# Reordering the end of block 0 in a retention + feed-forward kernel: weight loads, held input loads, a state moved between engines, and one state earlier in block 2

## The chip, the core and the metric

The kernel runs on one core of one Trainium2 chip. The metric is the device time of one execution in microseconds. The core has TensorE (matmuls; PE in the profile, PEld for its weight loads), VectorE (DVE), ScalarE (ACT), GpSimd (POOL), and SyncE (SP), which here only issues transfers.

## What is computed

Eight batches of retention (attention with a decaying causal weight in place of a softmax), followed by a feed-forward layer with a "snake" activation over all 4608 tokens:

```python
scores = scale * np.matmul(q, k.transpose(0, 1, 3, 2))      # (8, 8, 576, 576), head size 64
Dmat = np.where(rel >= 0, gamma[:, None, None] ** rel[None, :, :], 0.0)
ret = scores * Dmat[None, :, :, :]
attn = np.matmul(ret, v)                                     # -> x: (4608, 512)
h = x @ w_in                                                 # 512 -> 2048
s = np.sin(alpha * h)
g = h + s * s / (alpha + 1e-09)
out = g @ w_out                                              # 2048 -> 512
```

Inputs and output are float32; the kernel computes its products in float16 and adds in float32.

## The kernel before, in words

**Attention of a batch `b` (class `Attention`).** The first 512 of a batch's 576 positions are taken in two parts p of 256 positions, each of two chunks of 128. For each part q, k and v are loaded (`load`, 512 KB each, issued by SyncE), scaled by the decay and cast to float16 (`cast`, L181 for q and k, L104 or L102 for v), and q and k are transposed, either by TensorE (`turn`, L215, into a PSUM bank) with a copy out of the bank (`take`, L102/L104), or by a transfer (`crossed`, L205, issued by SyncE). Inside a chunk the kernel forms decayed scores (`scores`, L363; `masked`, L375, on VectorE) and multiplies them by v (`values`, L406). Across chunks it carries a state: `outer` (L298) forms k-times-v sums in a bank, `evict`, `evict_bank` or `take_sum` (L102/L104) copies them to the float32 tile `kvs`, `more(c)` (L344, L345, two GpSimd instructions) adds the decayed sum before to the sum c, and `to_state(c)` (L332) makes the float16 state that `add_states` (L428) multiplies by q. `next_sum` (L327), four VectorE instructions that decay and add straight out of the bank, stands in the class and isn't used before the change. The tile `kvs` has a single buffer for all batches: batch 4's sums can't be copied in before batch 3's last state is read. `keep` (L102/L104) writes the result as x, transposed, to the tile `xT`.

**Feed-forward of a block n (512 tokens, mostly batch n).** `project(n, fc)` (L541) makes 128 of the 2048 hidden features in a PSUM bank, four matmuls of 512 columns, or eight of 256 when it is called for halves. `sine` (L549, ScalarE), `square` (L558 on ScalarE, L560 on the others) and `product` (L565, VectorE) turn it into the tile `gT`; `product` is the last reader of the bank. `gemm2(n, u)` (L587) makes a quarter `u % 4` of the second product for 128 tokens `u // 4`: four matmuls that need four features of `gT` and quarter `u % 4` of w_out. `finish` copies the result out (`osb`) and stores it. From block 2 on the second product is formed with seven products of halves instead of eight (class `Quarters`, L658), for which `weigh` (L608, GpSimd) adds and subtracts halves of w_out beforehand.

**What sets the order.** The program is written out by hand, and each engine runs its instructions in that order, waiting on semaphores for what they read and for buffers to come free. The order of blocks 0 to 2 is a list of calls (L747 to L1271); later blocks are a loop. PSUM has the banks `h0`, `h1`, `h2`, `op` (one bank each) and `m0`, `m1` (two each). A tag names the bank that a call takes, and the call waits until the last user has read it. `told(instruction, engine)` puts a no-operation into an engine's queue that waits for that instruction; all that is behind it on the engine waits too. `relay=A_` of `values` does the same on ScalarE between two groups of matmuls that write different rows of one bank.

w_in and w_out come by four transfers each, issued by GpSimd (`load_w_in`, `load_w_out`, L92 and L95), which also cast them to float16. The stretch around the change: block 0's features 0 to 15 are projected from 17.5 to 33.2 us, its second product stands between batch 1's attention from 33.2 to 51.9, and block 1's projections begin at 51.9 with the rest of block 0's second product and batch 2's attention in between. `raw` float32 tiles rotate through six buffers, so that a load of batch 2 also waits for the cast of the same place in batch 1.

Of the kernel before, what the change touches and what calls it, by code (L numbers as in the profile page):

```python
# [18 lines left out]
def kernel(  # L19
# [16 lines left out]
    nc = tc.nc  # L36
# [57 lines left out]
    def load_w_out(g):  # L94
        nc.gpsimd.dma_start(w_out16[:, 4 * g : 4 * g + 4, :], w_out_r[:, 4 * g : 4 * g + 4, :])  # L95
# [42 lines left out]
    def cast(b, nm, p, eng, ys=(0, 1)):  # L138
        t_ = raw[b, nm, p]
        if (b, nm, p) not in half:  # L140
            if p < 2:
                if nm == "k":
                    d_ = work.tile([P, 16 * D], F16, tag=f"k16{slot(b, p)}", bufs=1, name="k16")
                elif nm == "q":
                    n = order_of_q.index((b, p)) % 3 if b < 5 else 1 - p
                    d_ = work.tile([P, 16 * D], F16, tag=f"q16{n}", bufs=1, name="q16")
                else:
                    d_ = work.tile([P, 16 * D], F16, tag="v16", bufs=4, name="v16")
                d_ = (
                    d_.rearrange("p (h r d) -> p h r d", r=2, d=D)  # L150
                    if nm == "v"
                    else d_.rearrange("p (a r t d) -> p a r t d", a=4, r=2, t=2)
                )
            elif nm == "v":
                d_ = work.tile([P, H, D], F16, tag="vs16", bufs=B // 2, name="vs16")
            else:
                tag, n = ("qks16", 2) if b % 4 == 0 else (f"k16{int(nm == 'q')}", 1)
                d_ = work.tile([P, 4, 2, D], F16, tag=tag, bufs=n, name=nm + "s16")
            half[b, nm, p] = d_
        dst = half[b, nm, p]  # L160
        if p == 2:
            if nm == "v":
                copy(eng, dst.rearrange("p h d -> p (h d)"), t_.rearrange("p h d -> p (h d)"))
            else:
                eng.tensor_tensor(
                    dst.rearrange("p a t d -> p t a d"),
                    t_.rearrange("p (t a) d -> p t a d", t=2),
                    fac_s[nm].rearrange("p (t a) -> p t a", t=2).unsqueeze(3).to_broadcast([P, 2, 4, D]),
                    MULT,
                )  # L170
        elif nm == "v":
            h0, h1 = 4 * ys[0], 4 * ys[-1] + 4
            copy(
                eng,
                dst[:, h0:h1].rearrange("p h r d -> p (h r d)"),
                t_[:, h0:h1].rearrange("p h x -> p (h x)"),
            )
        else:
            a0, a1 = 2 * ys[0], 2 * ys[-1] + 2
            n = 2 * (a1 - a0)  # L180
            return eng.tensor_tensor(  # L181
                dst[:, a0:a1].rearrange("p a r t d -> p t (a r) d"),
                t_.rearrange("p (t a) x -> p t a x", t=2)[:, :, a0:a1].rearrange("p t a (r d) -> p t (a r) d", r=2),
                fac["halved k" if nm == "k" and b >= HALVED else nm]
                .rearrange("p (t x) -> p t x", t=2)[:, :, 2 * a0 : 2 * a1]
                .unsqueeze(3)
                .to_broadcast([P, 2, n, D]),
                MULT,
            )
# [19 lines left out]
    def turn(b, nm, p, tag, ys=(0, 1)):  # L209
        if (b, nm, p) not in trs:  # L210
            trs[b, nm, p] = psum.tile([P, 1024], F16, tag=tag, bufs=1, name="tr")
        tr, x = trs[b, nm, p], half[b, nm, p]
        for a in range(2 * ys[0], 2 * ys[-1] + 2):
            for r in range(2):
                matmul(  # L215
                    tr[:, 256 * a + 128 * r : 256 * a + 128 * r + 128],
                    x[:, a, r].rearrange("p t d -> p (t d)"),
                    ident,
                    start=(a == 0 and r == 0), stop=True, is_transpose=True, skip_group_check=True,
                )  # L220
# [312 lines left out]
    def project(n, fc, tag, part=None):  # L533

        if n not in gT:
            gT[n] = work.tile([P, 2, FC, 256], F16, tag="gT", bufs=2, name="gT")
        if (n, fc) not in hps_of:
            hps_of[n, fc] = [bank(tag), None]
        cols = PART[part]
        for a in range(KT):  # L540
            matmul(  # L541
                hps_of[n, fc][0][:, cols], w_in16[:, a, fc * P : (fc + 1) * P], xs[n][:, a, cols],
                start=(a == 0 and part != 1), stop=(a == KT - 1), skip_group_check=True,
            )

    def sine(n, fc):
        hps = hps_of[n, fc][0]
        s_t = work.tile([P, 512], F16, tag="s", bufs=4, name="s_t")
        nc.scalar.activation(  # L549
            s_t, hps, mybir.ActivationFunctionType.Sin, bias=0.0, scale=alpha_t[:, fc : fc + 1],  # L550
        )
        hps_of[n, fc][1] = s_t

    def square(n, fc, eng):
        s_t = hps_of[n, fc][1]
        ss_t = work.tile([P, 512], F16, tag="ss", bufs=4, name="ss_t")
        if eng is nc.scalar:
            nc.scalar.activation(ss_t, s_t, mybir.ActivationFunctionType.Square)  # L558
        else:
            eng.tensor_tensor(ss_t, s_t, s_t, MULT)  # L560
        hps_of[n, fc][1] = ss_t
# [184 lines left out]
    with tc.manual_schedule():  # L746
# [139 lines left out]
        project(0, 10, "m0")  # L886
        sine(0, 10)
        square(0, 10, G_)
        load_w_out(2)
        told(cast(1, "k", 0, V, (1,)), G_)  # L890
        project(0, 11, "op")
        sine(0, 11)
# [4 lines left out]
        sine(0, 12)  # L897
        square(0, 12, G_)
        project(0, 13, "h0")
        turn(1, "k", 0, "m1")  # L900
        take(1, "k", 0, V, (0,))
        take(1, "k", 0, V, (1,))
        sine(0, 13)
        square(0, 13, A_)
        cast(1, "q", 0, G_)
        product(0, 12)
        product(0, 13)
        project(0, 14, "h1")
        sine(0, 14)
        square(0, 14, A_)  # L910
        project(0, 15, "m0")
        sine(0, 15)
        product(0, 14)
        square(0, 15, A_)
        product(0, 15)
        gemm2(0, 4, "op")
        gemm2(0, 12, "h2")
        turn(1, "q", 0, "m1")
        take(1, "q", 0, A_, (0,))
        take(1, "q", 0, V, (1,))  # L920
        gemm2(0, 0, "h0")
        at[0].to_state(3, G_)
        at[1].scores(0, 0, "m0")
        at[1].scores(0, 1, "m1")
        at[1].masked(0, 0)
        at[1].masked(0, 1)
        gemm2(0, 5, "op")
        cast(1, "v", 0, G_, (0,))
        cast(1, "v", 0, A_, (1,))
        load_w_out(3)  # L930
        gemm2(0, 13, "h2")
        load(2, "k", 1)
        load(2, "k", 0)
        load(2, "q", 0)
        cast(1, "k", 1, G_)
        at[1].outer((0,), "m0")
        at[1].evict((0,), A_)
        at[1].values(0, False, "m1", relay=A_)
        at[1].to_state(0, G_)
        gemm2(0, 1, "h0")  # L940
        gemm2(0, 6, "op")
        turn(1, "k", 1, "h1")
        cast(1, "q", 1, V)
        take(1, "k", 1, V)
        at[1].values(0, True)
        at[1].add_states(0)
        at[1].keep(0, A_)
        load(2, "v", 0)
        load(2, "v", 1)
        load(2, "q", 1)  # L950
        turn(1, "q", 1, "m0")
        take(1, "q", 1, V)
        at[1].more(1)
        at[1].to_state(1, G_)
        weigh(1, 0, G_)
        cast(1, "v", 1, A_)
        gemm2(0, 8, "h1")
        at[1].scores(1, 1, "m0")
        at[1].scores(1, 0, "m1")
        at[1].masked(1, 1)  # L960
        at[1].masked(1, 0)
        cast(2, "k", 1, V)
        cast(2, "k", 0, V)
        crossed(2, 0, "k")
        gemm2(0, 9, "h1")
        gemm2(0, 14, "h2")
        gemm2(0, 2, "h0")
        at[1].outer((1,), "m0")
        at[1].evict((1,), A_)
        at[1].more(2)  # L970
        at[1].to_state(2, G_)
        at[1].values(1, False, "m1", relay=A_)
        gemm2(0, 10, "h1")
        gemm2(0, 15, "h2")
        finish(0, 3)
        gemm2(0, 7, "op")
        at[1].values(1, True)
        at[1].add_states(1)
        at[1].keep(1, A_)
        weigh(1, 1, G_)  # L980
        finish(0, 1)
# [531 lines left out]
```

## Time and profile before

| | |
|---|---|
| median of 3 runs | 296.5 us (296.3 to 296.61) |
| the profiled execution's own time | 296.5 us |
| its span (first to last instruction) | 294.8 us |
| granted TensorE clock | 0.997 |
| busy: TensorE, VectorE, ScalarE, GpSimd | 282.2, 218.1, 211.0, 208.9 us |
| HBM read and written | 36.74 MB, 9.44 MB |

Times in the text count from the start of the span. A row of the timeline has start, duration, engine, line, operation, output<-inputs, shape and count, and in brackets the idle time of the engine just before it and whose end ended that. Matmuls overlap, so that the next group can begin some 0.16 us before the end that a row shows. A row of the chain has start, duration and what was waited for.

### The profile page before, as it was taken

Reading aid. Unit: us, or ns where it says so; the run is one execution under the profiler, and the core shown is the slowest. Engines: PE = TensorE matmul, PEld = TensorE weight load, DVE = VectorE, ACT = ScalarE, POOL = GpSimd, SP = SyncE. Lnnn points to the kernel's source line nnn. Section 1 sums busy time; section 2 is a strip of 40 time slices with the busy share of each in tenths; the row PEclk is TensorE's granted clock in tenths of the full one; section 3 lists DMA queues with packets and bytes.
Section 4 is the critical chain, followed back from the end, with each engine's and each line's share of the span. In section 5 each row is a group of like instructions: output and inputs, shape, how many; then the busy total and the mean of one; then the engine's idle time right before and its main releaser. Section 6 shows DMA issues by size and latency. Waiting matters only on the chain.

```text
span 294.8 us, 8767 instructions
## 1 busy us (share of the span) xinstructions
PE 282.2 (96%) x3611; PEld 184.9 (63%) x3611; DVE 218.1 (74%) x294; ACT 211.0 (72%) x342; POOL 208.9 (71%) x201
## 2 busy tenths in 40 slices
PE   7699999999999899999999999999999999999993
PEld 5474454676644566676666666666666666665782
DVE  3759978599965799989686967686777495747861
ACT  2859823985959798787778778787868879887600
POOL 4888878999999989999997799679916800460000
PEclk9999999999999999999999999999999999999998
DMA  7999999999998787978799884778756101311225
GB/s 222 293 250 221 240 263 317 240 211 326 165 210 275 114 181 178 282 164 194 182 257 154 181 231 115 93 162 181 141 125 162 38 3 38 72 38 26 59 47 119
DMA packets 119159, 49.89 MB, mean 169 GB/s; under 512 B 69824, under 2 KB 118096, under 8 KB 119120
## 3 DMA queue, kind: packets, MB, share of 16 engines
q1 hardware_dynamic: 114528, 45.04, 65.9%
q0 software_dynamic: 4224, 4.19, 8.5%
q8 instruction: 28, 0.46, 0.7%
q10 hardware_dynamic: 368, 0.11, 0.2%
q14 instruction: 11, 0.09, 0.1%
HBM read 36.74 MB, written 9.44 MB: 157 GB/s over the span
## 4 chain that ended last, share of the span: by engine, by line
PE 65%; POOL 17%; DMA 6%; DVE 5%; issue 2%; ACT 2%; SPq 0%; POOLq 0%; DVEq 0%; ACTq 0%
PE hps L541 29%; PE hps L658 29%; DMA q<-in_q_dram 6%; POOL T L608 5%; POOL q L181 3%; POOL kvs L345 2%; DVE gT L565 2%; PE sc L363 2%; POOL s L332 2%; POOL k L181 2%; PE o L406 2%; POOL s L344 1%; POOL v L104 1%; PE ops L587 1%; PE kv L298 1%
## 5 line engine op out<-in xcount | busy, mean ns | idle before, releaser
L565 DVE SCALAR_TENSOR_TENSOR gT<-ss_t,inva,hps 128x512 f16<-128x512 f16 x144 | 105.4, 744 | 42.1 <-ACT ss_t L558 40.1
L549 ACT ACTIVATE s_t<-hps,alpha_t 128x512 f16<-128x512 f32 x144 | 96.5, 681 | 37.3 <-PE hps L541 36.9
L541 PE MATMUL hps<-xT,w_in 128*128 128x512 f16 (+1 forms) x604 | 121.4, 347 | 1.3 <-ACT kvs L102 0.9
L541 PEld LDWEIGHTS <-w_in 128*128 128x128 f16 x668 | 63.6, 98 | 51.5 <-issue 2.0
L558 ACT ACTIVATE ss_t<-s_t 128x512 f16<-128x512 f16 x121 | 75.7, 630 | 3.4
L658 PEld LDWEIGHTS <-gT 128*128 128x128 f16 x656 | 63.9, 98 | 14.4
L630 POOL TENSOR_TENSOR gT<-gT,d 128x1024 f16<-128x1024 f16 x12 | 25.6, 2149 | 27.1 <-PE hps L658 25.7
L658 PE MATMUL hps<-T,gT 128*128 128x256 f16 x336 | 39.8, 273 | 0.0
L658 PE MATMUL hps<-w_out,gT 128*128 128x256 f16 x320 | 38.3, 273 | 0.0
L375 DVE TENSOR_TENSOR ret<-sc,mask 128x1024 f16<-128x1024 f32 (+1 forms) x32 | 35.1, 1119 | 2.6 <-PE sc L363 2.5
L678 DVE TENSOR_TENSOR osb<-osb,hps 128x512 f32<-128x512 f32 x35 | 23.9, 684 | 12.6 <-PE hps L658 11.9
L587 PE MATMUL ops<-w_out,gT 128*128 128x512 f16 x128 | 30.7, 380 | 0.1
L636 POOL TENSOR_TENSOR gT<-gT 128x1024 f16<-128x1024 f16 x12 | 25.3, 2127 | 0.0
L181 POOL TENSOR_TENSOR q<-q,cn 128x1024 f16<-128x1024 f32 (+1 forms) x16 | 25.2, 1589 | 0.1
L345 POOL TENSOR_TENSOR kvs<-s,kvs 128x256 f32<-128x256 f32 x24 | 19.8, 826 | 3.1 <-ACT kvs L102 1.3
L181 POOL TENSOR_TENSOR k<-k,cn 128x1024 f16<-128x1024 f32 (+1 forms) x11 | 19.2, 1748 | 2.8 <-DMA k<-in_k_dram 2.8
L587 PEld LDWEIGHTS <-gT 128*128 128x128 f16 x128 | 11.9, 98 | 13.4 <-DVE gT L565 0.9
L332 POOL TENSOR_TENSOR s<-kvs,cn 128x256 f16<-128x256 f32 x23 | 15.8, 687 | 4.9 <-ACT kvs L102 4.1
L102 ACT CAST xT<-o 128x1024 f16<-128x1024 f32 (+1 forms) x14 | 13.8, 989 | 5.9 <-PE o L428 5.9
L102 ACT COPY osb<-hps 128x512 f32<-128x512 f32 (+2 forms) x15 | 8.2, 549 | 13.5 <-PE hps L658 13.3
L344 POOL TENSOR_TENSOR s<-kvs,cn 128x256 f32<-128x256 f32 x24 | 16.6, 692 | 0.2
L560 DVE TENSOR_TENSOR ss_t<-s_t 128x512 f16<-128x512 f16 x16 | 11.5, 722 | 6.8 <-ACT s_t L549 6.8
(76 smaller groups left out, 274.2 us busy)
## 6 DMA issues: line engine op xcount, KB each, us to landing
out_dram<-osb SPq DMA_DIRECT2D x70, 128.0 KB, 2.5
q<-in_q_dram SPq DMA_DIRECT2D x16, 512.0 KB, 5.3
k<-in_k_dram SPq DMA_DIRECT2D x10, 512.0 KB, 6.6
v<-in_v_dram SPq DMA_DIRECT2D x10, 512.0 KB, 6.0
k<-in_k_dram SPq DMA_DIRECT2D x24, 128.0 KB, 3.6
v<-in_v_dram SPq DMA_DIRECT2D x24, 128.0 KB, 3.4
w_in<-in_moe_w_in_dram POOLq DMA_DIRECT2D x4, 512.0 KB, 9.4
w_out<-in_moe_w_out_dram POOLq DMA_DIRECT2D x4, 512.0 KB, 9.3
```

What stands on the lines that cost most here:

```text
L181: return eng.tensor_tensor(dst[:, a0:a1].rearrange("p a r t d -> p t (a r) d"), t_.rearrange("p (t a) x -> p t a x", t=2)[:, :, a0:a1].rea ...
L345: nc.gpsimd.tensor_tensor(self.kvs[:, c], s32, self.kvs[:, c], ADD)
L375: made = nc.vector.tensor_tensor(ret.rearrange("p t (z x) -> p (t z) x", z=2)[:, :, 0:n], sc.rearrange("p t (z x) -> p (t z) x", z=2)[:, : ...
L541: matmul(hps_of[n, fc][0][:, cols], w_in16[:, a, fc * P : (fc + 1) * P], xs[n][:, a, cols], start=(a == 0 and part != 1), stop=(a == KT - ...
L549: nc.scalar.activation(s_t, hps, mybir.ActivationFunctionType.Sin, bias=0.0, scale=alpha_t[:, fc : fc + 1],)
L558: nc.scalar.activation(ss_t, s_t, mybir.ActivationFunctionType.Square)
L565: nc.vector.scalar_tensor_tensor(gT[n][:, :, fc, :], ss_t.rearrange("p (t n) -> p t n", t=2), inva[:, fc : fc + 1], hps.rearrange("p (t n) ...
L587: matmul(ops[n, c, cols.start][:, cols], gT[n][:, c // 2, fk, c % 2 * P : c % 2 * P + P], w_out16[:, fk, cols], start=(fk == 0), stop=(fk ...
L630: eng.tensor_tensor(self.part(0, 0, i), self.part(1, 1, i), self.d3[:, 4 * i : 4 * i + 4], SUB)
L636: eng.tensor_tensor(out_, self.part(1, 0, i), self.part(0, 0, i), SUB)
L658: matmul(self.ps[name][:, 256 * m + cols.start : 256 * m + cols.stop], left(j)[:, P * m : P * m + P], right(j)[:, cols], start=(tag is not ...
L678: nc.vector.tensor_tensor(out_, a, self.ps[ps], ADD)
```

## The change

1. Block 0: w_out's quarter 2 (`load_w_out(2)`) moves on GpSimd from behind `square(0, 10)` to behind batch 1's first q cast; quarter 3 moves up to the same place, from behind batch 1's v cast.
2. Block 0: on TensorE the transposes of batch 1's k move behind projections 14 and 15 and a quarter of the second product; those of q behind two more quarters; the quarters after that are spread anew over batch 1's attention. Both halves of the copy of qT are ScalarE's now, `turn(1, "k", 1)` takes bank m0 instead of h1, and some of `gemm2`'s tags are the same banks at other places.
3. SyncE waits for the first mask of batch 1 (`told(at[1].masked(0, 0), nc.sync)`) before it issues batch 2's six loads; these are now all in one place.
4. Batch 1, part 1: instead of a copy of both sums by ScalarE and `more(2)`, `to_state(2)` on GpSimd, VectorE makes sum 2 from the bank (`next_sum(2)`) and state 2 (`to_state(2, V)`), and ScalarE copies sum 3 alone. `weigh(1, 1)` is earlier on GpSimd.
5. Batch 2: the output stores of block 0 come ahead of the transposes of k; the cast and the transpose of the first q, and the load of batch 3's first k, move behind `product(1, 0)`.
6. Block 2: `at[3].to_state(3)` on GpSimd moves ahead of the two casts of batch 4's q.

```diff
-        load_w_out(2)
         told(cast(1, "k", 0, V, (1,)), G_)
...
+        sine(0, 13)
+        square(0, 13, A_)
+        cast(1, "q", 0, G_)
+        load_w_out(2)
+        load_w_out(3)
+        product(0, 12)
+        project(0, 14, "h1")
+        sine(0, 14)
+        square(0, 14, A_)
+        product(0, 13)
+        project(0, 15, "m0")
+        sine(0, 15)
+        square(0, 15, A_)
+        gemm2(0, 4, "op")
         turn(1, "k", 0, "m1")
         take(1, "k", 0, V, (0,))
         take(1, "k", 0, V, (1,))
-        sine(0, 13)
-        square(0, 13, A_)
-        cast(1, "q", 0, G_)
-        product(0, 12)
-        product(0, 13)
-        project(0, 14, "h1")
-        sine(0, 14)
-        square(0, 14, A_)
-        project(0, 15, "m0")
-        sine(0, 15)
         product(0, 14)
-        square(0, 15, A_)
         product(0, 15)
-        gemm2(0, 4, "op")
         gemm2(0, 12, "h2")
+        gemm2(0, 0, "h0")
         turn(1, "q", 0, "m1")
         take(1, "q", 0, A_, (0,))
-        take(1, "q", 0, V, (1,))
-        gemm2(0, 0, "h0")
+        take(1, "q", 0, A_, (1,))
         at[0].to_state(3, G_)
+        gemm2(0, 5, "op")
+        gemm2(0, 13, "h2")
         at[1].scores(0, 0, "m0")
         at[1].scores(0, 1, "m1")
-        at[1].masked(0, 0)
+        told(at[1].masked(0, 0), nc.sync)
         at[1].masked(0, 1)
-        gemm2(0, 5, "op")
         cast(1, "v", 0, G_, (0,))
         cast(1, "v", 0, A_, (1,))
-        load_w_out(3)
-        gemm2(0, 13, "h2")
         load(2, "k", 1)
         load(2, "k", 0)
         load(2, "q", 0)
+        load(2, "v", 0)
+        load(2, "v", 1)
+        load(2, "q", 1)
+        gemm2(0, 1, "h0")
         cast(1, "k", 1, G_)
         at[1].outer((0,), "m0")
         at[1].evict((0,), A_)
+        at[1].to_state(0, G_)
+        gemm2(0, 8, "h1")
         at[1].values(0, False, "m1", relay=A_)
-        at[1].to_state(0, G_)
-        gemm2(0, 1, "h0")
-        gemm2(0, 6, "op")
-        turn(1, "k", 1, "h1")
         cast(1, "q", 1, V)
+        gemm2(0, 9, "h1")
+        turn(1, "k", 1, "m0")
         take(1, "k", 1, V)
...
+        weigh(1, 1, G_)
+        gemm2(0, 2, "h0")
+        gemm2(0, 10, "h1")
+        gemm2(0, 15, "h2")
+        at[1].outer((1,), "m0")
+        at[1].next_sum(2)
+        at[1].to_state(2, V)
+        at[1].take_sum(3, A_)
+        at[1].values(1, False, "m1", relay=A_)
+        gemm2(0, 7, "op")
+        finish(0, 3)
+        at[1].values(1, True)
+        at[1].add_states(1)
+        at[1].keep(1, A_)
+        finish(0, 1)
         cast(2, "k", 1, V)
         cast(2, "k", 0, V)
         crossed(2, 0, "k")
-        gemm2(0, 9, "h1")
-        gemm2(0, 14, "h2")
-        gemm2(0, 2, "h0")
-        at[1].outer((1,), "m0")
-        at[1].evict((1,), A_)
-        at[1].more(2)
-        at[1].to_state(2, G_)
...
-        cast(2, "q", 0, V)
-        crossed(2, 0, "q")
         crossed(2, 1, "k")
-        load(3, "k", 1)
...
         gemm2(0, 3, "h0")
         product(1, 0)
+        cast(2, "q", 0, V)
+        crossed(2, 0, "q")
+        load(3, "k", 1)
         finish(0, 0)
...
         cast(4, "k", 1, G_, (1,))
+        at[3].to_state(3, G_)
         cast(4, "k", 1, V, (0,))
...
         cast(4, "q", 0, G_, (1,))
-        at[3].to_state(3, G_)
```

VectorE, from the second products of block 0's last features to block 1's first ones. Before (`k_971`, `k_973`, `q_1101` are batch 2's casts; the numbers behind the names are those of tiles):

```order
L375 TENSOR_TENSOR ret<-sc,mask 128x1024 x2
L181 TENSOR_TENSOR k_971<-k_792,cn 128x2x8x64
L181 TENSOR_TENSOR k_973<-k_794,cn 128x2x8x64
L181 TENSOR_TENSOR q_1101<-q_796,cn 128x2x8x64
L560 TENSOR_TENSOR ss_t<-s_t 128x512
L565 SCALAR_TENSOR_TENSOR gT<-ss_t,inva,hps 128x2x256 x2
L560 TENSOR_TENSOR ss_t<-s_t 128x512
```

VectorE at the same place now, with `next_sum` (L327) and the state `s_846`:

```order
L375 TENSOR_TENSOR ret<-sc,mask 128x1024 x2
L327 SCALAR_TENSOR_TENSOR kvs<-kvs,cn,kv 128x64 x4
L332 TENSOR_TENSOR s_846<-kvs,cn 128x256
L181 TENSOR_TENSOR k_1097<-k_793,cn 128x2x8x64
L181 TENSOR_TENSOR k_1099<-k_795,cn 128x2x8x64
L560 TENSOR_TENSOR ss_t<-s_t 128x512
L565 SCALAR_TENSOR_TENSOR gT<-ss_t,inva,hps 128x2x256
L181 TENSOR_TENSOR q_1154<-q_797,cn 128x2x8x64
L565 SCALAR_TENSOR_TENSOR gT<-ss_t,inva,hps 128x2x256
L560 TENSOR_TENSOR ss_t<-s_t 128x512
```

Five instructions came in ahead of batch 2's k casts, and the q cast went from before block 1's first square to between products 0 and 1.

GpSimd in block 2, before (`k_1829`, `q_1831`, `k_1997`, `q_2007` are batch 4's casts, `sS` batch 3's last state):

```order
L181 TENSOR_TENSOR k_1829<-k_1657,cn 128x2x8x64
L181 TENSOR_TENSOR q_1831<-q_1671,cn 128x2x4x64 x2
L181 TENSOR_TENSOR k_1997<-k_1673,cn 128x2x4x64
L181 TENSOR_TENSOR q_2007<-q_1679,cn 128x2x4x64 x2
L332 TENSOR_TENSOR sS<-kvs,cn 128x256
L608 TENSOR_TENSOR T_2083<-w_out_72,T_1681 128x512 x2
```

GpSimd at the same place now:

```order
L181 TENSOR_TENSOR k_1831<-k_1659,cn 128x2x8x64
L181 TENSOR_TENSOR q_1833<-q_1673,cn 128x2x4x64 x2
L181 TENSOR_TENSOR k_1999<-k_1675,cn 128x2x4x64
L332 TENSOR_TENSOR sS<-kvs,cn 128x256
L181 TENSOR_TENSOR q_2010<-q_1681,cn 128x2x4x64 x2
L608 TENSOR_TENSOR T_2085<-w_out_72,T_1683 128x512 x2
```

The state passed the two halves of the q cast.

More of the change, by code (lines that the diff above doesn't have):

```diff
@@ L947 @@
         at[1].keep(0, A_)
[L948 to L952, printed above, removed]
         at[1].more(1)
@@ L956 @@
         cast(1, "v", 1, A_)
-        gemm2(0, 8, "h1")
+        gemm2(0, 6, "op")
+        turn(1, "q", 1, "m0")
+        take(1, "q", 1, V)
+        gemm2(0, 14, "h2")
         at[1].scores(1, 1, "m0")
@@ L964 @@
         crossed(2, 0, "k")
-        gemm2(0, 9, "h1")
-        gemm2(0, 14, "h2")
-        gemm2(0, 2, "h0")
-        at[1].outer((1,), "m0")
-        at[1].evict((1,), A_)
-        at[1].more(2)
-        at[1].to_state(2, G_)
[L972 to L981, printed above, removed]
-        cast(2, "q", 0, V)
-        crossed(2, 0, "q")
         crossed(2, 1, "k")
-        load(3, "k", 1)
         at[1].more(3)
```

## The prediction

> **What bounds the kernel now.** I read the page first, then the chain of waits, then each engine's timeline at the places where the chain leaves TensorE.
>
> ```profile
> PE 282.2 (96%) x3611; PEld 184.9 (63%) x3611; DVE 218.1 (74%) x294; ACT 211.0 (72%) x342; POOL 208.9 (71%) x201
> PE 65%; POOL 17%; DMA 6%; DVE 5%; issue 2%; ACT 2%; SPq 0%; POOLq 0%; DVEq 0%; ACTq 0%
> ```
>
> TensorE is busy for 96% of the span, and its work isn't changed: only its pauses can be won, or new ones added. The second line (the chain by engine) says that 17% of the chain runs through POOL all the same. Rows of the chain in order of time, and of the timelines of TensorE, ScalarE and POOL (start, duration, engine, line; in brackets the idle time before and what ended it), show where POOL holds TensorE up late in block 2:
>
> ```profile
> 99.14 0.58 POOL sS L332
> ...
> 113.90 1.73 PE hps L541 x8
> ```
> ```profile
> 99.16 0.29 PE L428 MATMUL o<-qT,s 64*64 64x128 f16 x8
> 100.39 7.29 PE L541 MATMUL hps<-xT,w_in 128*128 128x512 f16 x52 [0.94 <-ACT kvs L102]
> 107.51 1.91 PE L658 MATMUL hps<-w_out,gT 128*128 128x256 f16 x16
> 109.56 1.92 PE L541 MATMUL hps<-xT,w_in 128*128 128x512 f16 x8
> ```
> ```profile
> 96.58 1.44 ACT L549 ACTIVATE s_t<-hps,alpha_t 128x512 f16<-128x512 f32 x2
> 99.75 0.59 ACT L102 COPY kvs<-kv 128x512 f32<-128x512 f32 x1 [1.73 <-POOL sS L332]
> ```
> ```profile
> 96.93 2.22 POOL L181 TENSOR_TENSOR q<-q,cn 128x512 f16<-128x512 f32 x2
> 99.11 0.61 POOL L332 TENSOR_TENSOR sS<-kvs,cn 128x256 f16<-128x256 f32 x1
> ```
>
> Read backwards: projection 5 waits 0.94 us for bank h0; ScalarE frees it by copying batch 4's sums at 99.75, after 1.73 us of idleness; it waits because `kvs` is one buffer, which batch 3's last state (POOL, `sS`, 99.11) still reads. In the chain's last row eight full matmuls take 1.73 us, 0.216 each: my price for TensorE's work (a projection, or a quarter of the second product, is four matmuls, 0.86). By it the 16 half-wide matmuls from 107.51 should hand over at 109.24; the next began at 109.56, and 0.32 more is lost.
>
> The end of block 0, on TensorE's timeline:
>
> ```profile
> 18.30 11.86 PE L541 MATMUL hps<-xT,w_in 128*128 128x256 f16 x68
> 30.63 0.40 PE L215 MATMUL tr<-ident,k 128*128 128x128 f16 x4 [0.47 <-DVE k L181]
> 31.23 0.40 PE L215 MATMUL tr<-ident,k 128*128 128x128 f16 x4 [0.20 <-DVE k L181]
> 31.47 1.89 PE L541 MATMUL hps<-xT,w_in 128*128 128x512 f16 x8
> ...
> 50.87 0.28 PE L428 MATMUL o<-qT,s 64*64 64x128 f16 x8
> 51.62 0.31 PE L428 MATMUL o<-qT,s 64*64 64x128 f16 x8 [0.47 <-POOL s L332]
> 51.86 2.21 PE L541 MATMUL hps<-xT,w_in 128*128 128x256 f16 x16
> ...
> 60.07 0.71 PE L298 MATMUL kv<-v,k 64*64 64x64 f16 x64
> ...
> 62.56 0.42 PE L363 MATMUL sc<-qT,kT 64*64 64x128 f16 x16
> ```
>
> Projections 0 to 13 end at 30.16 (the next could start some 0.16 earlier, at 30.0, since ends overlap), and the transposes of k run from 30.63 to 31.47; four of them take 0.24 when they are fed (31.23 to 31.47), so eight take 0.48 and 1.0 us is lost. At 50.87 the second state is late: the two groups of eight take 0.75 and 0.24, so 0.5 is lost. So some 1.5 us lie here and 1.4 in block 2; much more than 1% can't be won.
>
> **Part 1: block 0's order.** Projections 14 and 15 and one quarter of the second product now stand ahead of the transposes of k. What does 15 wait for? Its bank m0, which product 10 reads on VectorE:
>
> ```profile
> 29.57 1.60 DVE L181 TENSOR_TENSOR k<-k,cn 128x512 f16<-128x512 f32 x2
> 31.10 1.39 DVE L565 SCALAR_TENSOR_TENSOR gT<-ss_t,inva,hps 128x512 f16<-128x512 f16 x2
> ...
> 36.79 2.35 DVE L375 TENSOR_TENSOR ret<-sc,mask 128x1024 f16<-128x1024 f32 x2 [0.18 <-PE sc L363]
> ...
> 46.80 2.63 DVE L181 TENSOR_TENSOR k<-k,cn 128x1024 f16<-128x1024 f32 x2
> 49.36 1.73 DVE L181 TENSOR_TENSOR q<-q,cn 128x1024 f16<-128x1024 f32 x1
> ...
> 54.92 0.75 DVE L565 SCALAR_TENSOR_TENSOR gT<-ss_t,inva,hps 128x512 f16<-128x512 f16 x1
> 56.12 0.75 DVE L565 SCALAR_TENSOR_TENSOR gT<-ss_t,inva,hps 128x512 f16<-128x512 f16 x1 [0.45 <-ACT ss_t L558]
> 56.78 0.57 DVE L560 TENSOR_TENSOR ss_t<-s_t 128x512 f16<-128x512 f16 x1
> 57.46 1.41 DVE L565 SCALAR_TENSOR_TENSOR gT<-ss_t,inva,hps 128x512 f16<-128x512 f16 x2
> 58.78 0.68 DVE L104 COPY osb<-ops 128x512 f32<-128x512 f32 x1
> ```
>
> Product 10 is the first of the two at 31.10 and ends at 31.8; VectorE's order up to there is the same. Projection 14 ends at 30.87, so 15 waits 1.0 us: the loss at the transposes of k comes back whole at projection 15. From there I add up the new order by the prices above, with the row that frees each bank beside it: scores 38.1 to 38.7; first outer product at 39.8 (bank m0 is held by the first mask, half of the 2.35, from 38.5; 0.15 lost); second transposes of k at 42.35, of q at 44.1; second scores 45.6; second outer product 48.9; second values and one quarter to 50.45. What feeds that k comes from POOL:
>
> ```profile
> 38.89 1.89 POOL L181 TENSOR_TENSOR k<-k,cn 128x1024 f16<-128x1024 f32 x1 [2.80 <-DMA k<-in_k_dram]
> ...
> 50.09 1.48 POOL L332 TENSOR_TENSOR s<-kvs,cn 128x256 f16<-128x256 f32 x1
> ```
>
> The cast waits for its load, ends at 40.8 as before, and is 1.5 us early for its transposes.
>
> **Part 2: the second state by VectorE.** POOL loses `more(2)` and `to_state(2)`; VectorE gets four multiply-adds over 128x64 and one 128x256 product. The trace has neither on VectorE. Bounds of a multiply-add: nothing, and the 0.75 of the 128x512 one (56.12); it has an eighth of the columns, so I take 0.2. The product is at most half a cast half (29.57: 1.60 for two, so 0.4). The outer product lands at 49.35; 49.4 + 0.8 + 0.4 is 50.6, and TensorE wants the state at 50.5. At the upper end, 3 us for the four, TensorE would wait 2.2 more. With the state's own matmuls (0.24 and the switch) block 1's first projection starts at 51.1 instead of 51.86: 0.75 won.
>
> POOL's `s` at 50.09 began beside VectorE's q cast (49.36 to 51.09), and took 1.48 instead of the 0.61 of the `sS` row. The Trainium skill (SBUF — State Buffer, Who interferes with whom) says that a VectorE instruction with two SBUF inputs and a GpSimd one that reads SBUF exclude each other. The trace agrees: the `s` ends 0.48 after the cast. By that rule batch 1's first state, due on POOL at 41.0 just behind the start of another q cast of VectorE, would end at some 43.2, when TensorE wants it, and the sum would be smaller by 0.1; without it nothing changes.
>
> **Part 3: a q cast between two products.** The cast of batch 2's first q (1.73) moves behind product 0 of block 1, ahead of product 1. Product 0, 0.8 sooner, runs from 54.1 to 54.85; cast to 56.5; product 1 to 57.15 (before 56.87); square 2 to 57.65; products 2 and 3 to 59.1; output copy to 59.7 (before 59.46). Projection 6 wants product 2 (58.45) at 58.3, and batch 2's outer product the copy's bank at 59.3. So that outer product starts at 59.8 instead of 60.07: of the 0.75, **0.3** is left. The cover is used up here; each further tenth on VectorE comes off the sum.
>
> **Part 4: the loads.** On SyncE batch 2's six loads wait for the first mask; behind them stand output stores and batch 2's transposes. On POOL w_out's last two quarters go out at 34.2 and 35.0, behind the q cast, with a state and the casts of v and k behind them.
>
> ```profile
> 30.18 5.13 SPq L121 DMA_DIRECT2D v<-in_v_dram  x1
> 35.40 5.92 SPq L121 DMA_DIRECT2D k<-in_k_dram  x2
> ...
> 49.57 2.83 SPq L205 DMA_TRANSPOSE kT<-k  x1
> ```
> ```profile
> w_out<-in_moe_w_out_dram POOLq DMA_DIRECT2D x4, 512.0 KB, 9.3
> ```
> ```profile
> kT<-k SPq DMA_TRANSPOSE x2, 5.4
> ```
>
> Issues of 512 KB that take 3 to 5 us are pushed back by a full queue: batch 1's transfers are still in it at 35.4 (POOL's cast waits until 38.89 for one). The mask ends at 39.7, so the hold is 4.3 us. Bounds: nothing, if the queue stays full meanwhile, or 4.3 us of lateness for six loads; I take nothing, because of these long issues. VectorE's casts of batch 2's k start at 50.6 now, 3.8 later than at 46.80, so they hide most of it. With the 9.3 us from issue to landing of the page, w_out's quarters land at 43.5 and 44.3; they are wanted at 43.2 and 47.9. So between nothing and 0.3; nothing, since the earlier quarters queued behind others for part of the 9.3.
>
> **Part 5: block 2.** `to_state(3)` of batch 3 passes two q casts, 2.22 us (96.93), and would run at 96.9; POOL's earlier loss of two instructions comes on top. ScalarE's copy then follows its sines at 98.0, and the bank is free at 98.6, before TensorE comes at 99.1: the 0.94 goes, and 0.15 of slow start behind it. The q casts end 0.6 later; their transposes have until the scores behind 109.56. What is late next?
>
> ```profile
> 100.90 0.75 DVE L565 SCALAR_TENSOR_TENSOR gT<-ss_t,inva,hps 128x512 f16<-128x512 f16 x1 [1.87 <-ACT ss_t L558]
> ...
> 108.10 2.30 DVE L565 SCALAR_TENSOR_TENSOR gT<-ss_t,inva,hps 128x512 f16<-128x512 f16 x3
> ```
>
> VectorE stood behind the same ScalarE copy (1.87 idle), and the second of the three products at 108.10 frees bank h2 at 109.5, for the matmuls of 109.56. VectorE starts 1.8 sooner, TensorE arrives 1.4 sooner: the 0.32 goes too. Sum of the block: 0.94 + 0.15 + 0.32 = **1.4**.
>
> **Sum.** The profiled execution took 296.5 (294.8 of span, 1.7 around it), which is the median too. 0.3 + 1.4 = 1.7 off: **294.8 us**.
>
> **Rivals.**
> 1. *VectorE doesn't eat block 0's gain.* For it: the idle 0.45 ahead of product 1; against it: part 3's full schedule. All 0.75 stays, with the multiply-adds at their lower bound 0.2 more: 296.5 - 0.95 - 1.4 = 294.15. Chance 0.14.
> 2. *Block 2 stays late.* If ScalarE is the limit there by its own work, only block 0's 0.3 to 0.5 comes out: 296.1. Its 1.73 of idleness speaks against. Chance 0.14.
> 3. *The held loads come late: slower.* If the hold empties the queue, all six land 4.3 later, and batch 2's transposes are issued beside loads, 2.83 each as at 49.57: k0 at 54, k1 at 56.8, q0 at 59.6, landing 5.4 later at 65.0. TensorE wants the scores at 62.3 (before 62.56), so 2.7 is lost against 1.7 won: 297.5. It decides from the moment when q0's transpose lands after 62.3, and is slower from 64.0. The long issues speak against. Chance 0.11.
> 4. *The change doesn't do what it says.* The order of every engine shows that it does; no chance of its own.
>
> **How the numbers follow.** Forecast 0.61 (294.3 to 295.7, by tenths on VectorE), rivals 0.14, 0.14, 0.11. The range, 294.0 to 296.4, takes in the first two rivals and leaves out the third and the upper bound of the multiply-adds. A measurement of this kernel tells 0.2%, 0.6 us, from no change. Faster, below 295.9: forecast, first rival and a little of the second, 0.76. Same: most of the second, 0.13. Slower: 0.11.
>
> **What would show it.** Right: no wait of ScalarE's `kvs` copy for `sS` near 98, and projection 5 directly behind the states; about 1 us of waiting for VectorE ahead of projection 15 near 31; the second state within 0.3 of its reader; batch 2's outer product right behind VectorE's output copy. Wrong: batch 2's scores waiting for a transpose, a multiply-add of over 0.3, or a pause between 62 and 98 that eats the lead.

## The result and the profile after

The changed kernel took **295.0 us** (median of 6 runs, 294.37 to 295.61), the kernel before 296.56 beside it (6 runs, 296.3 to 296.96): a ratio of **0.9945, 95% interval 0.9927 to 0.9963**. The profiled execution took 295.11, with a span of 293.4 (before: 296.5 and 294.8).

The page after, busy time and the chain by engine:

```profile
PE 281.2 (96%) x3611; PEld 184.5 (63%) x3611; DVE 218.2 (74%) x298; ACT 211.0 (72%) x343; POOL 209.0 (71%) x198
PE 81%; POOL 7%; DVE 4%; issue 2%; ACT 2%; DMA 2%; DVEq 0%; ACTq 0%; POOLq 0%
```

Busy times are nearly the same; POOL's share of the chain fell from 17% to 7%. TensorE's timeline of the changed kernel, from block 0 to batch 3:

```profile
18.30 12.73 PE L541 MATMUL hps<-xT,w_in 128*128 128x256 f16 x72
31.89 1.02 PE L541 MATMUL hps<-xT,w_in 128*128 128x512 f16 x4 [0.86 <-DVE gT L565]
...
51.13 2.21 PE L541 MATMUL hps<-xT,w_in 128*128 128x256 f16 x16
...
58.88 1.05 PE L541 MATMUL hps<-xT,w_in 128*128 128x256 f16 x8 [0.34 <-DVE gT L565]
60.14 0.72 PE L298 MATMUL kv<-v,k 64*64 64x64 f16 x64 [0.21 <-DVE osb L104]
...
78.30 0.76 PE L298 MATMUL kv<-v,k 64*64 64x64 f16 x64
79.46 0.42 PE L363 MATMUL sc<-qT,kT 64*64 64x128 f16 x16 [0.41 <-DMA qT<-q]
```

Projection 15 waits for VectorE at 31, and block 1 begins at 51.13 instead of 51.86: 0.73 won, as forecast. But batch 2's outer product stands at 60.14, where it was at 60.07 before: TensorE waited for VectorE's products and output copy, and all of the 0.73 is gone. At 79.46 it waits once more, for a transpose of batch 3.

Block 2, on TensorE, POOL and ScalarE after:

```profile
99.40 0.29 PE L428 MATMUL o<-qT,s 64*64 64x128 f16 x8
99.61 7.13 PE L541 MATMUL hps<-xT,w_in 128*128 128x512 f16 x52
...
108.33 1.97 PE L541 MATMUL hps<-xT,w_in 128*128 128x512 f16 x8
```
```profile
96.56 0.61 POOL L332 TENSOR_TENSOR sS<-kvs,cn 128x256 f16<-128x256 f32 x1
97.13 2.22 POOL L181 TENSOR_TENSOR q<-q,cn 128x512 f16<-128x512 f32 x2
```
```profile
98.28 0.58 ACT L102 COPY kvs<-kv 128x512 f32<-128x512 f32 x1
```

The state stands ahead of the q casts and runs at 96.56 instead of 99.11. ScalarE's copy has no idle time before it any more, and projection 5 begins 0.21 behind the states, without the 0.94. At 97.45 TensorE was 0.23 behind the kernel before (97.22), at 108.33 it is 1.23 ahead (109.56): block 2 gave 1.46.

**What ate the lead.** VectorE and POOL of the changed kernel between 49.5 and 60:

```profile
49.52 0.86 DVE L327 SCALAR_TENSOR_TENSOR kvs<-kvs,cn,kv 128x64 f32<-128x64 f32 x4 [1.05 <-PE kv L298]
50.41 0.42 DVE L332 TENSOR_TENSOR s<-kvs,cn 128x256 f16<-128x256 f32 x1
50.76 1.63 DVE L181 TENSOR_TENSOR k<-k,cn 128x1024 f16<-128x1024 f32 x1
...
52.31 1.74 DVE L181 TENSOR_TENSOR k<-k,cn 128x1024 f16<-128x1024 f32 x1
53.98 0.83 DVE L560 TENSOR_TENSOR ss_t<-s_t 128x512 f16<-128x512 f16 x1
54.92 0.75 DVE L565 SCALAR_TENSOR_TENSOR gT<-ss_t,inva,hps 128x512 f16<-128x512 f16 x1
...
59.40 0.68 DVE L104 COPY osb<-ops 128x512 f32<-128x512 f32 x1
```
```profile
41.02 1.45 POOL L332 TENSOR_TENSOR s<-kvs,cn 128x256 f16<-128x256 f32 x1 [2.29 <-ACT kvs L102]
...
50.46 0.85 POOL L344 TENSOR_TENSOR s<-kvs,cn 128x256 f32<-128x256 f32 x1 [1.47 <-DVE kvs L327]
51.39 1.59 POOL L345 TENSOR_TENSOR kvs<-s,kvs 128x256 f32<-128x256 f32 x1
53.05 1.48 POOL L332 TENSOR_TENSOR sS<-kvs,cn 128x256 f16<-128x256 f32 x1
54.48 3.23 POOL L104 CAST v<-v 128x1024 f16<-128x1024 f32 x2
```

Put the ends beside each other. POOL's L344 ends at 51.31, VectorE's first k cast, begun at 50.76, at 52.39; POOL's L345, begun at 51.39, at 52.98; the second k cast at 54.05; POOL's `sS` at 54.53; the square at 54.81. From the end of the other engine's instruction the rest takes 1.08, 0.59, 1.07, 0.48 and 0.28. It looks as if the two engines take turns, each instruction held until the other's is over. No row shows idle time: the waiting is inside the duration.

VectorE has no slack here: from 50.76 to the copy's end at 60.08 there is hardly a gap, so what its casts lose TensorE loses at 60. Not all of the 0.73 goes this way: the forecast had only 0.3 of it left, for the five new instructions and the moved q cast. Experiment 4 tells the two shares apart.

### The profile page after: what moved, and what is told of

The parts are those of the page before. It is cut to its first block, busy times and chain, and to the rows that moved or that the text cites. A ratio compares the mean times of both kernels' runs of the same rounds, so it can differ in the third digit from the quotient of the medians.

```text
span 293.4 us, 8769 instructions
## 1 busy us (share of the span) xinstructions
PE 281.2 (96%) x3611; PEld 184.5 (63%) x3611; DVE 218.2 (74%) x298; ACT 211.0 (72%) x343; POOL 209.0 (71%) x198
## 4 chain that ended last, share of the span: by engine, by line
PE 81%; POOL 7%; DVE 4%; issue 2%; ACT 2%; DMA 2%; DVEq 0%; ACTq 0%; POOLq 0%
PE hps L541 35%; PE hps L658 29%; PE ops L587 7%; PE sc L363 2%; POOL T L608 2%; PE o L406 2%; DVE gT L565 2%; DMA qT<-q 2%; PE idle L702 1%; PE kv L298 1%; DVE ret L375 1%; PE tr L215 1%; POOL kvs L345 1%; POOL q L181 1%; POOL v L104 1%
## 5 line engine op out<-in xcount | busy, mean ns | idle before, releaser
L345 POOL TENSOR_TENSOR kvs<-s,kvs 128x256 f32<-128x256 f32 x23 | 19.3, 839 | 1.8
L344 POOL TENSOR_TENSOR s<-kvs,cn 128x256 f32<-128x256 f32 x23 | 16.1, 698 | 1.6 <-DVE kvs L327 1.5
L102 ACT COPY kvs<-kv 128x512 f32<-128x512 f32 (+2 forms) x15 | 8.1, 546 | 9.6 <-DVE kvs L327 5.0
```

Of the source, the lines that this page charges most:

```text
L102: eng.copy(d_, s_)
```

## The experiments

Executions begin block 0's long run of projections (18.30 in both kernels' profiles) between 18.03 and 20.83, by what comes ahead of it; "aligned" times below have that difference taken off, so that they can be set beside 18.30. The medians have that difference in them. "Behind" and "ahead" are TensorE's. Theories A to W2 are named in the expectations.

**1. The parts apart.** e1 is the kernel before with block 2's edit alone, e2 the change without it.

```diff
 e1 (on before), the reverse in e2 (on the changed kernel)
-at[3].to_state(3, G_)        # behind cast(4, "q", 0, G_, (1,))
+at[3].to_state(3, G_)        # behind cast(4, "k", 1, G_, (1,))
```

> The kernel before with the move in block 2 alone (batch 3's last state ahead of the two casts of batch 4's q). Theory A, the parts add up and block 2 carries nearly all: 1.3 to 1.5 us faster than before, about as fast as the whole change; ScalarE's copy of batch 4's sums no longer waits for the state near 98, and the three losses of 0.94, 0.15 and 0.32 us go together. Rival B, the move needs block 0's lead to pay: under 0.7 us faster, with a new wait of TensorE for VectorE's products near 107.

> The changed kernel with the state of block 2 back at its old place, so the parts of block 0 and block 1 alone. Theory A: within 0.3 us of the kernel before; TensorE leads by 0.7 us at 51 and has lost it again at 60; the 0.9 us wait ahead of projection 5 of block 2 is there. Rival B: over 0.5 us faster than before, since GpSimd's two instructions less bring the state early enough.

e1: 295.59 (12 runs, lowest 294.96), ratio 0.9966 [0.9942, 0.999]. e2: 296.46 (12 runs, lowest 295.69), 0.9988 [0.9976, 1.0]. The kernel before beside them: 296.71, lowest 295.99. TensorE at the end of e1's block 2, and of e2's:

```profile
101.02 0.29 PE L428 MATMUL o<-qT,s 64*64 64x128 f16 x8
101.24 7.13 PE L541 MATMUL hps<-xT,w_in 128*128 128x512 f16 x52
```
```profile
100.95 7.29 PE L541 MATMUL hps<-xT,w_in 128*128 128x512 f16 x52 [0.68 <-ACT kvs L102]
```

From those last state matmuls to the end of the span: before 294.8 - 99.16 = 195.6, e1 295.2 - 101.02 = 194.2. So the move wins its 1.4 without block 0's lead (1.1 by the medians): A holds, B falls. (e1's profiled execution, 296.9, waited 1.81 for a q cast at 43.9, which its edit doesn't touch.) In e2 the wait is there, with 0.68. Block 0's part alone is worth 0.25 by the medians, which its interval hardly tells from nothing. The two ratios multiply to 0.9954, beside 0.9945 for the whole.

**2. VectorE's state.** The old lines for the second state in the new order:

```diff
-at[1].next_sum(2)
-at[1].to_state(2, V)
-at[1].take_sum(3, A_)
+at[1].evict((1,), A_)
+at[1].more(2)
+at[1].to_state(2, G_)
```

> The changed kernel with batch 1's second state by GpSimd again, from ScalarE's copy of both sums. Theory C: TensorE waits 0.7 to 1.2 us for the state near 51, but VectorE's k casts end 1.5 us or more sooner, so that the waits near 59 go: within 0.4 us of the changed kernel. Rival E, VectorE's state is worth what it wins at 51: 0.7 us or more slower than the changed kernel, with TensorE still behind by as much at 60.

298.18 (6 runs), ratio 1.004 [1.0025, 1.0055], 3 us above the changed kernel. TensorE and POOL:

```profile
52.83 0.31 PE L428 MATMUL o<-qT,s 64*64 64x128 f16 x8 [1.94 <-POOL s L332]
```
```profile
48.83 1.59 POOL L344 TENSOR_TENSOR s<-kvs,cn 128x256 f32<-128x256 f32 x1
50.50 1.58 POOL L345 TENSOR_TENSOR kvs<-s,kvs 128x256 f32<-128x256 f32 x1
```

E holds, at a higher price than either side expected: POOL's two instructions stand beside VectorE's k casts and take 1.59 and 1.58 instead of 0.61 and 0.73. Without VectorE's state the new order would have made the kernel slower.

**3. A k cast sooner.**

```diff
+cast(2, "k", 1, V)
 at[1].outer((1,), "m0")
...
-cast(2, "k", 1, V)
```

> The changed kernel with VectorE's cast of batch 2's k of part 1 moved up, behind the second mask and ahead of the second outer product's sums, into 1.05 us of VectorE's idle time in which GpSimd idles too. Theory C, the lead of 0.7 us at 51 is lost because VectorE's two k casts stand ahead of block 1's first square and take 3.3 us beside GpSimd instead of 2.6: product 0 of block 1 comes 0.8 us sooner, the waits of TensorE of 0.5 and 0.4 us near 59 go, and the run is 0.4 to 0.8 us faster than the changed kernel. Rival D, the q cast between products 0 and 1 is what eats it: the waits near 59 stay within 0.2 us, and the run is within 0.2 us of the changed kernel.

296.76 (12 runs), ratio 1.0007 [0.9993, 1.0021]. VectorE and TensorE (0.23 to add for alignment):

```profile
48.16 1.69 DVE L181 TENSOR_TENSOR k<-k,cn 128x1024 f16<-128x1024 f32 x1
```
```profile
60.10 1.05 PE L541 MATMUL hps<-xT,w_in 128*128 128x256 f16 x8 [1.32 <-DVE gT L565]
```

C's forecast failed as it was put. GpSimd wasn't idle yet: the early cast took 1.69 all the same, now beside POOL's combination of w_out, which ran until 48.77. The squares, pushed beside POOL's casts, took 1.25 and 1.47, POOL's q cast 2.88, and batch 2's outer product came at 61.58 aligned, 1.4 behind the changed kernel. Rival D's forecast failed as well, since the wait near 60 grew to 1.32. To move one instruction only changes which pair meets. So the next experiment takes the meeting away.

**4. POOL waits for the k casts.**

```diff
-cast(2, "k", 0, V)
+told(cast(2, "k", 0, V), G_)     # ahead of at[1].more(3) on POOL
```

> The changed kernel in which GpSimd waits for VectorE's second k cast of batch 2 before it forms batch 1's last sum and state and casts v and q, so that the two engines don't work at once between 50.8 and 53.4. Theory C (the lead of 0.73 is lost because the k casts are stretched beside GpSimd): the two k casts take 2.6 instead of 3.37, product 0 begins at 54.0 to 54.2 instead of 54.92, and batch 2's outer product at 59.4 to 59.8 instead of 60.14 if GpSimd's v casts, now 1 later, end by 58.8: 294.5 to 294.9. Rival D (the q cast between the products eats the lead): product 0 sooner, but the outer product at 60.1 or later, 295.0.

295.33 (12 runs), ratio 0.9946 [0.9922, 0.997]. VectorE, TensorE and POOL (0.20 to add for alignment):

```profile
50.55 2.35 DVE L181 TENSOR_TENSOR k<-k,cn 128x1024 f16<-128x1024 f32 x2
...
54.05 0.75 DVE L565 SCALAR_TENSOR_TENSOR gT<-ss_t,inva,hps 128x512 f16<-128x512 f16 x1
...
73.70 2.26 DVE L181 TENSOR_TENSOR k<-k,cn 128x512 f16<-128x512 f32 x1
```
```profile
18.10 12.73 PE L541 MATMUL hps<-xT,w_in 128*128 128x256 f16 x72
...
59.64 0.72 PE L298 MATMUL kv<-v,k 64*64 64x64 f16 x64 [0.21 <-DVE osb L104]
...
77.82 1.05 PE L541 MATMUL hps<-xT,w_in 128*128 128x256 f16 x8 [0.98 <-DVE xT L104]
```
```profile
73.52 1.90 POOL L181 TENSOR_TENSOR q<-q,cn 128x1024 f16<-128x1024 f32 x1
```

Alone, the two k casts take 2.35 together (1.22 each, the rows overlap) instead of 3.29. Product 0 begins at 54.25 aligned (the prediction: 54.1) and the outer product at 59.84 (59.8): with the meeting gone, part 3's numbers come true. That they do so this closely is in part chance: the q cast still stands beside POOL's state and v cast and takes 1.59 (1.22 in the changed kernel, where POOL waits for it), and the forecast had priced it at 1.73 by a row of before that held a wait too. Of the 0.73 won at 51, 0.23 is left at 60, so the meetings cost 0.30 and the other 0.5 is what part 3 had forecast. C holds for this stretch, D falls. But the time, 295.33, isn't the forecast 294.5 to 294.9: the lead is lost at the next meeting: VectorE's cast of batch 3's k begins at 73.70, 0.18 behind POOL's q cast, and takes 2.26, which is 1.72 to the end of POOL's instruction at 75.42, and 0.54. The copy behind it (`keep`) comes late, and TensorE waits 0.98.

What the rows show, the Trainium skill states as a rule (SBUF — State Buffer, Who interferes with whom): VectorE's second input from SBUF comes through a port shared with GpSimd, an exclusive lock, where the other side blocks. By that rule VectorE's products and output copy, with one SBUF input or none beside PSUM, should not be touched; the trace agrees, 0.75 and 0.68 in both kernels and here.

**5. Where the q cast stands, and a square for POOL.**

```diff
 e7: directly behind the k casts on VectorE, as in before; e10: the same, and
-square(1, 0, V)
+square(1, 0, G_)              # behind to_state(3), ahead of the v casts
```

> The changed kernel with the cast of batch 2's first q back in its old place on VectorE, directly behind the two k casts and ahead of the first product of block 1. Theory C (VectorE is full from 50.8 to 60.1, and what counts is the sum of its work, stretched beside GpSimd): product 0 begins near 57 instead of 54.9, the last copy still ends at 60.1, and batch 2's outer product begins within 0.3 of 60.1; 295.0, within 0.4. Rival D (the place of the q cast is what eats the lead or saves it): TensorE waits at projection 5 for product 0's bank and at projection 6 as well, the outer product begins 0.5 to 1 later, 295.6 to 296.

> The changed kernel with block 1's first square on GpSimd (behind the last state, ahead of the v casts) and the q cast of batch 2 directly behind the k casts on VectorE, so that VectorE has 0.83 less to do between 50.8 and 60.1. Theory C (VectorE is what bounds that stretch): its last copy ends at 59.3 instead of 60.08 and batch 2's outer product begins at 59.4; the time falls to 294.3 to 294.7 unless the lead is lost again behind 70. Rival G (the square and the q cast hold each other up, since both engines read from SBUF): GpSimd's square takes 1.8 instead of 1.04, product 0 begins at 56.4 or later, the outer product at 60.1 or later, 295.0 or slower.

e7: 297.2 (12 runs, lowest 296.82), ratio 1.002 [0.9988, 1.0052]. VectorE and TensorE (2.53 to take off; the profiled execution, 300.97, is 3.8 above the median):

```profile
58.07 1.25 DVE L560 TENSOR_TENSOR ss_t<-s_t 128x512 f16<-128x512 f16 x1
...
60.74 1.62 DVE L560 TENSOR_TENSOR ss_t<-s_t 128x512 f16<-128x512 f16 x1
```
```profile
63.27 1.65 PE L541 MATMUL hps<-xT,w_in 128*128 128x256 f16 x8 [2.02 <-DVE gT L565]
```

The sum of VectorE's work isn't all that counts: in the old place the q cast pushes both squares beside POOL's casts (0.83 and 0.60 become 1.25 and 1.62), and TensorE waits 2.02 at projection 6. Product 0 begins at 56.89 aligned, as C had it, but the outer product at 62.31 instead of 60.1. So D is right that the place matters, by 2 us and not by 0.5 to 1, though through the same meetings. e10: 295.41 (12 runs), 0.9939 [0.9915, 0.9963], no gain. POOL and TensorE:

```profile
54.26 2.02 POOL L560 TENSOR_TENSOR ss_t<-s_t 128x512 f16<-128x512 f16 x1
```
```profile
59.42 1.05 PE L541 MATMUL hps<-xT,w_in 128*128 128x256 f16 x8 [1.12 <-DVE gT L565]
```

Rival G holds: POOL's square, beside VectorE's q cast, takes 2.02 (1.04 in block 0), and product 0 waits for it.

**6. The loads.** e5 takes the hold out, e6 loads w_out's last quarters at their old places; e12 is the changed kernel again, beside e6 and e11.

```diff
 e5
-told(at[1].masked(0, 0), nc.sync)
+at[1].masked(0, 0)
 e6
+load_w_out(2)                 # behind square(0, 10, G_)
+load_w_out(3)                 # behind cast(1, "v", 0, A_, (1,))
-load_w_out(2)                 # behind cast(1, "q", 0, G_)
-load_w_out(3)
```

> The changed kernel without the hold: SyncE issues batch 2's six loads as soon as their buffers are free (from about 35), not behind the first mask at 39.8. Theory H (the prediction's part 4: the hold costs nothing and gives nothing, since the queue is full meanwhile): TensorE's block 1 begins at 51.1 and batch 2's outer product at 60.1, both within 0.3 of the changed kernel, and the time is 295.0, within 0.3. Rival W (the hold clears the way for batch 1's loads and for the second half of w_out): k of batch 1's second part lands at 38.8 again instead of 35.8, w_out's third quarter after 43.2, where TensorE wants it, and TensorE waits 0.5 to 1.5 between 42 and 48: 295.5 to 296.5.

> The changed kernel with w_out's last two quarters loaded at their old places in GpSimd's order (the third ahead of batch 1's q cast, the fourth behind the cast of v). Theory of part 4 (w_out's delay costs nothing and gives nothing): k of batch 1's second part lands some 3 later than 35.8, GpSimd's cast of it ends at 40.8 and is still early for its transposes; block 1 begins at 51.1 within 0.2, 295.0 within 0.4. Rival W2 (GpSimd lives on the earlier k: without it the first state comes later): TensorE waits at the first state, 44 to 45, by 0.3 to 1, block 1 begins at 51.4 to 52.1.

> The changed kernel itself once more, on the same chip as the two others, so that their times can be set beside it: 295.0, within 0.4; batch 2's outer product at 60.14, and the scores of batch 3 wait 0.4 to 0.6 for a transpose at 79 if that wait isn't chance.

e5: 294.45 (9 runs), ratio 0.991 [0.9879, 0.994]. e6: 295.43 (6 runs), 0.9956 [0.994, 0.9972]. e12: 294.45 (6 runs), 0.9934 [0.9919, 0.9949]. H holds for the order of events, if not for its 295.0: without the hold SyncE issues batch 2's first k at 31.64 aligned, with it at 39.81, and it lands at 45.83 and at 45.84 (the last load, q, at 53.34 and 54.83, before GpSimd casts it at 57.67); in e5 and e12 block 1 begins at 51.13 aligned and the outer product at 60.13, as in the first profile. W2 falls too: 51.14 in e6. Rival W and the theory for e6 both had batch 1's k land 3 later; it lands at 35.18 in e5 and 36.16 in e6 (38.81 before, 35.77 in the changed kernel), so what brought it forward stays open.

By the medians e6 is 1.0 slower than e12 beside it. No row shows where: with the difference at the start taken off, the profiled spans are 293.0 in both, 293.1 in e5 and 293.4 in the first profile.

e12's profile (0.90 to take off):

```profile
19.20 12.73 PE L541 MATMUL hps<-xT,w_in 128*128 128x256 f16 x72
...
61.03 0.71 PE L298 MATMUL kv<-v,k 64*64 64x64 f16 x64 [0.21 <-DVE osb L104]
...
79.18 0.76 PE L298 MATMUL kv<-v,k 64*64 64x64 f16 x64
79.76 0.40 PE L363 MATMUL sc<-qT,kT 64*64 64x128 f16 x16
...
97.73 0.81 PE L298 MATMUL kv<-v,k 64*64 64x64 f16 x64
```

Here batch 3's scores don't wait: 78.86 aligned, against 79.46 in the first profile and 79.25 before. So the wait for the transpose at 79 comes in some executions and not in others. At 97.73, 96.83 aligned, TensorE is 0.39 ahead of before (97.22), in the first profile 0.23 behind; in e5 and e6 it is 0.36 and 0.37 ahead there, in e2 0.17. This is what block 0's part gave, between -0.2 and +0.4. It isn't the lead of 51, which is gone at 60. VectorE's square and POOL's combination of w_out near 66, before and then after:

```profile
65.81 1.27 DVE L560 TENSOR_TENSOR ss_t<-s_t 128x512 f16<-128x512 f16 x1
```
```profile
64.54 2.25 POOL L608 TENSOR_TENSOR T<-T,w_out 128x512 f16<-128x512 f16 x2
```
```profile
65.89 0.81 DVE L560 TENSOR_TENSOR ss_t<-s_t 128x512 f16<-128x512 f16 x1
```
```profile
64.15 2.26 POOL L608 TENSOR_TENSOR T<-T,w_out 128x512 f16<-128x512 f16 x2
```

In both kernels the square ends 0.29 behind POOL's instruction (66.79 and 66.41). POOL, with three instructions less, is 0.38 sooner, and between 65 and 71 TensorE goes from 0.08 behind the kernel before to 0.25 ahead of it (its scores stand at 70.75 and 70.50). So the meetings can also give a lead. The rows fit this; no run tested it.

**7. Two more meetings removed.** Both stand on experiment 4's kernel.

```diff
 e11
-cast(3, "k", 0, V, (0,))      # ahead of product(1, 13) and keep
 at[2].keep(0, V)
+cast(3, "k", 0, V, (0,))
 e13
-weigh(2, 0, G_)               # ahead of batch 2's states on POOL
+weigh(2, 0, G_)               # behind batch 3's q casts
```

> The run before last (GpSimd held behind the k casts) with one more move: VectorE's cast of the first half of batch 3's k stands behind its copy of batch 2's output (keep) instead of ahead of it, so that the copy, which TensorE waited 0.98 for at 77.8, doesn't stand behind a cast that waits for GpSimd's q cast (2.26 instead of 1.26). Theory C (VectorE's casts and squares and GpSimd's instructions exclude each other, and each lead gained is lost wherever the next pair meets): TensorE passes 77 without a wait, the outer product of batch 3 begins at 77.8 instead of 78.79, and the time is 294.2 to 294.6 by an undisturbed execution, 0.4 to 1.0 below the changed kernel. Rival K (something else, such as the transposes of batch 3, stands behind the copy at 79): the scores wait there instead, 295.0.

> GpSimd held behind VectorE's k casts of batch 2, as in that earlier run, and one of GpSimd's three combinations of w_out (two instructions, 2.26 together, at 64.7) stands behind batch 3's q casts instead of ahead of batch 2's states, so that GpSimd's cast of batch 3's q is over by 72 and no longer meets VectorE's k cast at 73.7. Theory C (what is gained is lost wherever VectorE's cast or square next meets a GpSimd instruction): VectorE's k cast takes 0.6 to 1.2 instead of 2.26, the 0.98 of TensorE's wait at 77.8 goes, batch 3's scores begin at 78.4 to 78.7 instead of 79.38, and the fastest executions take 294.0 to 294.2, 0.2 to 0.3 below the changed kernel's. Rival M (another pair meets instead: GpSimd's v casts wait for their loads until 73.6 and stand beside the same k cast): a wait of 0.3 to 1.0 stays between 75 and 79, and the time is the changed kernel's, 294.4 or more.

e11: 295.16 (6 runs), ratio 0.9955 [0.9941, 0.997]. e13: 295.16 (5 runs), 0.995 [0.993, 0.997]. VectorE's cast and TensorE in e13 (aligned within 0.01):

```profile
73.93 0.99 DVE L181 TENSOR_TENSOR k<-k,cn 128x512 f16<-128x512 f32 x1
```
```profile
77.86 0.71 PE L298 MATMUL kv<-v,k 64*64 64x64 f16 x64
79.44 0.42 PE L363 MATMUL sc<-qT,kT 64*64 64x128 f16 x16 [0.87 <-DMA qT<-q]
```

The meeting with the q cast is gone (0.99 instead of 2.26; the cast now meets POOL's second v cast, which ends at 74.38), and batch 3's outer product begins at 77.86, 0.44 sooner than in the changed kernel; but now the scores wait 0.87 for the transpose. Rival M's time and wait come, if not for its reason. In e11 one cast of k meets POOL's second v cast and the other POOL's `more`, and TensorE stops 0.18 inside the outer product; the scores don't wait there, so rival K's wait is seen in e13 and not in e11. C holds for each meeting, and its times fail. No version here beats the changed kernel: with the difference at the start taken off, the profiled spans are 293.8 (e9), 293.7 (e10), 293.3 (e11) and 293.4 (e13), against 293.4 and 293.0 in the changed kernel's two profiles.

## Why the prediction was right, point by point

- **Part 1, right.** Projection 15 waits 0.86 for VectorE (forecast 1.0, counted from start to start). The first outer product (39.80), the transposes of k and q (42.37, 44.24) and the second outer product (48.91) come within 0.15 of the forecast. POOL's k cast came 2 sooner than forecast, its load having landed at 35.77, and nothing followed from that.
- **Part 2, right.** Four multiply-adds take 0.86, a product 0.42 (taken: 0.8 and 0.4), block 1 begins at 51.13 (51.1). Experiment 2 prices the alternative at 2 us there.
- **Part 3, the step that failed.** "Of the 0.75, 0.3 is left" priced VectorE's casts by rows of before: product 0 "from 54.1", the outer product "at 59.8". They came at 54.92 and 60.14. The two k casts took 3.29 instead of the 2.63 of before, and the square behind them 0.83 instead of 0.42; the q cast, priced at 1.73, took 1.22 and gave 0.5 of that back. Part 2 had named the very mechanism, for one state at 41.0 (it came: 1.45 instead of 0.61, hidden), but the new neighbours of the k casts were not looked up in POOL's order. Experiment 4 shows it: with the meeting taken away both numbers come within 0.15. The 0.3 came from elsewhere where it came: in e12 the lead grew from -0.06 at 60 to 0.39 at 97.
- **Part 4, right.** Hold and w_out cost TensorE nothing (e5, e6).
- **Part 5, right.** 1.46 against 1.4, and alone in e1. POOL's lead over before was only 0.37 by then (its cast of batch 3's q at 73.02 against 73.39), and that was enough.
- **Rivals.** 2 fell with e1, and 3 with the first profile (batch 2's scores stand at 62.64, 62.56 before, without a wait) and with e5. The first rival's time, 294.15, is near the lowest runs (294.3), but not by its mechanism: VectorE did eat the lead of block 0.

The total was right because block 2's 1.4 is nearly all of it. The term of 0.3 is luck where it fits: the lead it counted was lost, and another came near 66. The first profile also has one of the prediction's own signs of being wrong, the pause at 79 that eats a lead. Open is why batch 3's transpose lands late in some executions: `kT`, just ahead of `qT` in the queue, took 3.5 from issue to landing in e12 and 5.7 in the first profile, but also 5.3 in e5, where the scores don't wait. No run told these apart.

## What to carry to other kernels

When a change moves an instruction of VectorE with two inputs in SBUF, or any work of GpSimd, look up what the other engine does at the new time before you take a duration from the old trace: a duration there may hold a wait, or lack one that will come. Holding GpSimd back by a no-operation (`told`) gave the stretch its forecast times in experiment 4, but it made GpSimd later for all that followed, and the kernel as a whole was no faster. So before you count a lead as won, follow it to the next place where something else, here a transpose, is only just in time.

## What the runs showed of the hardware

Two engines that meet show no idle time, only longer instructions: the same 128x1024 cast on VectorE took 1.22 alone (experiment 4), 1.63 and 1.74 beside GpSimd in the changed kernel; a 128x512 cast 0.68 alone (before, at 30.50) and up to 2.26 (experiment 4); a 128x512 square 0.42 alone (before, at 158.22) to 1.62 (e7); GpSimd's 128x256 state 0.61 to 1.48. VectorE's products and its copies out of a bank kept their times beside the same instructions (0.75, 0.68). A multiply-add over 128x64 on VectorE is issued every 0.20.
